# A retention step's products issued in two parts around the up products (retention, ELU layer and gated layer on one core)

## The chip, the core and the metric

One core of a Trainium2 chip runs the whole program. The metric is the device time of one execution in microseconds; the time before is the median of three runs. The engines are TensorE (PE, with its weight loads as PEld), VectorE (DVE), ScalarE (ACT), GpSimd (POOL) and SyncE (SP), which issues the DMAs. Each takes its instructions in the order in which the program issues them.

## What is computed

```python
# retention: 4 sequences, 8 heads, 576 positions, 64 wide
scores = q @ k.T / sqrt(64)
ret = scores * Dmat            # Dmat[i, j] = gamma_h ** (i - j) for i >= j, else 0
x = (ret @ v)                  # heads side by side: 2304 tokens x 512
# first layer, 512 -> 2048 -> 512
h = x @ w_in
x = where(h > 0, h, exp(min(h, 0)) - 1) @ w_out
# second layer, 512 -> 1536 -> 512
out = (sigmoid(x @ w_gate) * (x @ w_val)) @ w_o2
```

All is 32-bit. Products of the two layers are made of three products of high and low parts; those of the retention are plain 32-bit products.

## The kernel before

The retention runs in 18 steps (`NSTEP`), 9 for each pair of sequences: four chunks of 128 positions of one sequence, four of the other, and a last step that holds the last 64 positions of both. `c` is the chunk's number in its sequence; `last` marks steps 8 and 17. A step holds all eight heads, and a chunk is worked as two halves of 64 positions (`X`), so that every product is 64 x 64 x 64, four of which fit on PE side by side. In the class `Step`:

- `load` fetches q, k and v of a step (one DMA; six DMAs for a last step), `scale` (line 256, POOL) multiplies v by the decay.
- `scores` (PE, 32 products into the PSUM tile `ts`), `causal` (line 271, DVE) masks them into `a`.
- `sums` (PE, 32 products of k and v into the first 256 columns of the PSUM tile `to`; none in a last step), `states` (lines 292 to 297: two adds on DVE, or a copy on ACT and an add, then a scaling on POOL) makes of them the state for the next step.
- `inter` (PE, 32 products of a state and q into the other 256 columns of `to`; 16 where `c` is 0) and `outs` (PE, 32 products of `a` and v, added onto them) give the step's outputs. All small products are issued at line 259. `inter` issues its halves in two orders, and after its first half a no-op on SP (line 312, `swept`) waits for that half; the first product that adds onto it waits for the no-op.
- `x_scaled` (line 331 on DVE out of `to`, then a cast on ACT, line 336) and `x_low` (line 339 on DVE) give the high and low part of x for 128 tokens; `x_low` also issues on SP the DMA that keeps x (line 343).

`block(n)` writes out the order for step n: state products of n, scores of n + 1, outputs of n, sums of n + 1, the mask, the loads of a later step (`loads_at`; step 13 issues step 17's six), the scaling of the outputs, the states of n + 1, the scaling of v of n + 2, and x's low part.

The first layer begins beside it. Its stage loop runs s = 0, 1, ...; for s below 18 a pass works 256 tokens (two steps) against one 128-wide part of the hidden layer. `ups` (class `FF`) makes the hidden values: 12 products of 128 x 128 x 256 into the PSUM tile `h` (line 358), two ACT operations (lines 369, 370), one on DVE (line 373), a cast on ACT and the low part on POOL (lines 107, 108). `downs`, two passes later, adds them into `acc` (12 products, lines 112 to 114); every second pass the sums are copied out (line 407). A pass with even s takes x of steps s and s + 1 and the next pass the same two; and from s = 4 to 15 `block(s + 2)` stands ahead of `ups`. The calls of `stage()` run, in passes 6, 9, 12, 15 and 16, the conversion of a weight in pieces: ACT lines 152 and 153 at the top, DVE lines 155 and 156 behind the up products, DVE line 159 behind the two ACT operations, DVE line 161 in the down products, and a cast (ACT) and a subtraction (POOL) at the top of the next pass. The order on each engine is the order of these calls; nothing plans it otherwise.

Of the kernel before, what the change touches and what calls it, by code (L numbers as in the profile page):

```python
# [19 lines left out]
B, H, S, D = 4, 8, 576, 64  # L20
# [9 lines left out]
NSTEP = (B // 2) * NS  # L30
# [10 lines left out]
AHEAD = 2  # L41
LATE = 4
# [10 lines left out]
def retention_elu_glu(  # L53
# [25 lines left out]
    class Ring:  # L79
# [5 lines left out]
        def more(self, pool, n):  # L85
            self.homes += [(pool, f"{self.name}{len(self.homes) + i}") for i in range(n)]
# [29 lines left out]
    def warm_up(n):  # L116

        h = h_bank()
        for i in range(n):
            pe.matmul(h[:, :256], warm[:, :128], warm, start=True, stop=True)  # L120

    def after(ins, other):

        tc.add_manual_dep(ins.ins, other.ins.name, mybir.DependencyInfo(
            mybir.DependencyClass.Sync, mybir.DependencyReason.DATA), reason="row tiles")
        return ins
# [8 lines left out]
    class Weight:  # L135
# [3 lines left out]
        def load(self, raw=None):  # L139
            self.ours = raw is None  # L140
            self.raw = raw_free.popleft() if self.ours else raw
            sp.dma_start(out=self.raw, in_=self.src.bitcast(I32))
# [76 lines left out]
    class Step:  # L219
# [51 lines left out]
            dve.tensor_tensor(out=self.a, in0=ts[:, :, : NP * HC].rearrange("j h (p i) -> j h p i", p=NP),  # L271
                              in1=tri.unsqueeze(1).unsqueeze(1).to_broadcast([128, 2, NP, HC]), op=ALU.mult)

        def sums(self, start=False):

            if self.last:
                return
            for p in range(NP):
                for h in range(2):
                    for X in range(2):  # L280
                        r, d = slice(64 * X, 64 * X + 64), slice(64 * h, 64 * h + 64)
                        self.mm(to[d, X, D * p : D * p + D], self.k[r, p, d], self.v[r, p, d], start and p == 0)

        def states(self):

# [60 lines left out]
    class FF:  # L346
# [41 lines left out]
        def downs(self, stage):  # L388
            sums, n = self.sums(), self.n
            g, w = [self.gt[:, i, :n] for i in range(2)], W["o", self.f].w  # L390
            for i, a in enumerate(sums):
                c = slice(i * 128, i * 128 + 128)
                mm3(a, w[:, 0, c], w[:, 1, c], *g, self.first and not (self.half and i % 2), self.last, self.half)
                if i == len(sums) // 2 - 1:
                    stage()
            if self.last:
                self.evac(sums)
# [373 lines left out]
    with tc.manual_schedule():  # L771
# [8 lines left out]
        to = ps_r.tile([128, 2, 512], F32, name="to")  # L780
# [12 lines left out]
        steps = [Step(n) for n in range(NSTEP)]  # L793
# [6 lines left out]
        for X in range(2):  # L800
            r = slice(64 * X, 64 * X + 64)
# [17 lines left out]
        loads_at = {}  # L819
# [3 lines left out]
        def block(n):  # L823

            more = n + 1 < NSTEP
            steps[n].inter()
            if more:
                steps[n + 1].scores()
            steps[n].outs()
            if more:  # L830
                steps[n + 1].sums()
                steps[n + 1].causal()
            for load in loads_at.get(n, []):
                load()
            steps[n].x_scaled()
            if more:
                steps[n + 1].states()
                if n + 2 < NSTEP:
                    steps[n + 2].scale()
            steps[n].x_low()  # L840

        def stages(chain, n):
            for _ in range(n):
                next(chain)
# [5 lines left out]
        steps[0].scores()  # L850
        steps[0].causal()
        warm_up(WARM[1])
        steps[0].sums(True)
        steps[0].states()
        steps[1].scale()
        stages(w0, 1)
        steps[0].inter()
        steps[1].scores()
# [4 lines left out]
        for load in loads_at[0]:  # L863
            load()
        steps[0].x_scaled()
        stages(w2, 1)
        stages(w0, 1)
        steps[0].x_low()
        stages(w0, 2)
# [21 lines left out]
        for i, w in enumerate(weights[4:8]):  # L891
            s = a + 6 + (i * (b - a - 6)) // 4
# [30 lines left out]
        def park():  # L923
            for g in (2, 3):
                parked_y[g] = dpool.tile([128, KB * N[g]], F32, tag=f"y{g}", name="y")
                sp.dma_start(out=parked_y[g], in_=y_of[g])
            two, t = (ypool.tile([128, 2048], I32, tag=f"y{g}", name="more") for g in (2, 3))
            more_raws[:] = two[:, :1024], two[:, 1024:]
            extra.update({3 + i: t[:, i * DM : i * DM + DM] for i in range(3)})
            raw_shut.clear()  # L930
            raw_free.extend(more_raws)
# [36 lines left out]
        def convert(w, **engines):  # L968

            name = name_of[id(w)]  # L970
            last = 2 if isinstance(w, Sums) else 4
            for n, _ in enumerate(w.chain(**engines)):
                if n == 3 and w not in weights[:7]:
                    more()
                if n == last and w not in weights[:8]:
                    done.append([name, 3])
                yield
# [8 lines left out]
        def save(all_=False):  # L986
            for d in done:
                d[1] -= 1
            while done and (all_ or done[0][1] < 0):
                n = done.pop(0)[0]  # L990
                w = W[n].w
                copies[n] = dpool.tile(list(w.shape), F32, tag="".join(map(str, n)), name="c")
                sp.dma_start(out=copies[n], in_=w.bitcast(F32))
# [42 lines left out]
        for s in range(end):  # L1036
            if halves is not None:
                next(halves, None)
            chain = halves = None
            if s in conv:  # L1040
                chain = halves = made[name_of[id(conv[s])]] = convert(conv[s])
                if conv[s] is W["i", 2 * Q0 + 2]:
                    halves = None

            def stage():
                if chain is not None:
                    next(chain, None)
                if s >= begins[1] + 4:
                    next(prepared, None)
            stage()  # L1050
            if LATE <= s < NSTEP - AHEAD:
                block(s + AHEAD)
            ff[s].ups(stage, s)
            if s == 0:
                steps[2].scores()
                steps[2].sums(True)
                steps[2].causal()
                steps[2].states()
                steps[3].scale()
            if s == 1:  # L1060
                block(2)
                warm_up(WARM[4])
                block(3)
                warm_up(WARM[5])
                for _ in weights[1].chain(dve):
                    pass
            if 1 < s < LATE:
                block(s + AHEAD)
            for w in loads.get(s, []):
                w.load()  # L1070
            if s >= LAG:
                ff[s - LAG].downs(stage)
            else:
                stage()
            save()
            for i, n in enumerate(("11", "21", "22")):
                if s == begins[1] + 2 + i:
                    second.store(n)
            if s == begins[1] + 8:
                park()  # L1080
                more()
            if s == begins[1] + LAG - 1:
                ret.close()
                right = ctx.enter_context(tc.tile_pool(name="right", bufs=1, side="right"))
                e_tile.more(right, 3)
                e_tile.n = 5
                g_tile.more(right, 2)
                t_tile.more(right, 1)
                s_tile = Ring("s", right, 2, [128, 2, 2, DM], F32R)
                ps_acc = ctx.enter_context(tc.tile_pool(name="ps_acc", bufs=1, space=bass.MemoryType.PSUM))  # L1090
                ps_u = ctx.enter_context(tc.tile_pool(name="ps_u", bufs=1, space=bass.MemoryType.PSUM))
                acc_bank = Ring("acc", ps_acc, 4, [128, 512], F32)
                u_bank = Ring("u", ps_u, 2, [128, 512], F32)
# [79 lines left out]
        for pair in (first, second):  # L1173
# [3 lines left out]
            for q in range(Q0, QN):  # L1177
                hooks = {}
                calls = 7 + len(todo) + (not last_q)
                if not last_q:  # L1180
# [3 lines left out]
                    if q == QN - 1:  # L1184
                        reload(second.sums)
                        restore(("i", 2 * Q0), ("i", 2 * Q0 + 1), ("z", Q0))
                        p = second
# [8 lines left out]
                else:  # L1196
# [10 lines left out]
                    back = [("o", 2 * q), ("o", 2 * q + 1)]  # L1207
# [36 lines left out]
        for which, pair in enumerate(pairs):  # L1244
            for f in range(FB):
# [11 lines left out]
                back = [(n, f + 1) for n in "vgs" if f + 1 < FB and (which or f + 1 in EARLY)]  # L1257
# [28 lines left out]
                if which and f == 2:  # L1286
                    free.extend((8, 9))
                    two = y_tile(4).rearrange("p (i t) -> p i t", i=2)
# [70 lines left out]
def build(nc, arrays):  # L1359
    args = [  # L1360
        nc.dram_tensor(f"in_{n}", a.shape, mybir.dt.from_np(a.dtype), kind="ExternalInput").ap()
        for n, a in arrays.items()
    ]
    args.append(nc.dram_tensor("out_0", (NT, DM), F32, kind="ExternalOutput").ap())
    with tile.TileContext(nc) as tc:
        retention_elu_glu(tc, *args)
# [12 lines left out]
```

## Time and profile before

| | |
|---|---|
| median of three runs | 895.14 us (895.12 to 895.22) |
| the profiled execution | 894.47 us, of which the span of the profile is 892.7 us |
| PE busy | 864.8 us (97%), 6430 matmuls |
| DVE, ACT, POOL busy | 670.0, 460.0, 411.0 us |
| chain that ended last | PE 77%, DVE 11%, ACT 4%, DMA 3%, issue 2%, POOL 1% |

Times in the profile are microseconds from the start of its span. A row gives a start, a length, the engine, the line, what is written and read, and how often; in brackets stands how long the engine had been idle and who released it. "Issue" is time in which an engine waited for nothing that the profile shows.

### The profile page before, as it was taken

To read this page: it belongs to the slowest core of one execution; us is meant where nothing else is said; L and a number is where in the kernel's file an instruction comes from. 1 tells how busy PE (TensorE), PEld (TensorE's weight loads), DVE (VectorE), ACT (ScalarE), POOL (GpSimd) and SP (SyncE) were. 2 spreads that over 40 slices of the span, in tenths; PEclk is the share of its full clock that TensorE was granted. 3 is DMA by queue.
4 is the path that set the end of the run, shared out by engine and by line. 5 is a ranking of instruction groups with operands and counts; after the bars stand their busy time and mean duration, and the time that the engine had idled before them with its cause. 6 is when DMAs were issued, how large, how long until landed. Compare 5 with 4: busy or idle time off the path is not lost.

```text
span 892.7 us, 16282 instructions
## 1 busy us (share of the span) xinstructions
PE 864.8 (97%) x6430; PEld 733.3 (82%) x6430; DVE 670.0 (75%) x971; ACT 460.0 (52%) x829; POOL 411.0 (46%) x327
## 2 busy tenths in 40 slices
PE   7899999999999999999999999999999999999998
PEld 5788888878888888888778788888887888888886
DVE  4767758679999977887886989579966654786675
ACT  2344566467667655666564665455534335343331
POOL 2255635545466643565541556245434243434353
PEclk9999999999999999999999999999999999999999
DMA  9976627934655496889782666545564565554332
GB/s 340 263 241 208 184 87 245 368 118 141 203 199 213 167 407 251 307 331 336 270 310 96 258 221 225 213 171 190 205 245 180 186 208 220 212 189 189 119 118 94
DMA packets 63868, 194.83 MB, mean 218 GB/s; under 512 B 9904, under 2 KB 19120, under 8 KB 57392
## 3 DMA queue, kind: packets, MB, share of 16 engines
q1 hardware_dynamic: 62384, 192.30, 60.5%
q10 hardware_dynamic: 1408, 1.49, 0.5%
q8 instruction: 50, 0.82, 0.4%
q14 instruction: 26, 0.21, 0.1%
HBM read 127.19 MB, written 66.58 MB: 217 GB/s over the span
## 4 chain that ended last, share of the span: by engine, by line
PE 77%; DVE 11%; ACT 4%; DMA 3%; issue 2%; POOL 1%; ACTq 0%; SPq 0%; DVEq 0%; POOLq 0%
PE u L112 12%; PE u L113 12%; PE u L114 12%; PE acc L112 8%; PE acc L113 8%; PE acc L114 8%; PE tile L112 3%; PE tile L113 3%; PE tile L114 3%; PE to L259 3%; PE h L358 2%; DVE y L442 2%; DMA y<-y 1%; DVE t L155 1%; DVE t L159 1%
## 5 line engine op out<-in xcount | busy, mean ns | idle before, releaser
L108 POOL TENSOR_TENSOR g<-e,g 128x512 fp32r<-128x512 f32 x95 | 133.3, 1408 | 225.2 <-ACT g L107 200.4
L112 PE MATMUL u<-x,s 128*128 128x512 f32 x288 | 114.5, 398 | 2.8 <-ACT u L492 1.7
L114 PE MATMUL u<-x,s 128*128 128x512 f32 x288 | 114.0, 396 | 0.0
L113 PE MATMUL u<-x,s 128*128 128x512 f32 x288 | 113.6, 395 | 0.0
L112 PE MATMUL u<-x,w 128*128 128x512 f32 (+1 forms) x264 | 98.8, 374 | 3.9 <-DVE e L512 2.5
L113 PE MATMUL u<-x,w 128*128 128x512 f32 (+1 forms) x264 | 98.4, 373 | 0.0
L114 PE MATMUL u<-x,w 128*128 128x512 f32 (+1 forms) x264 | 97.9, 371 | 0.0
L107 ACT CAST g<-e 128x512 fp32r<-128x512 f32 x101 | 61.8, 621 | 59.9 <-DVE e L567 37.9
L108 POOL TENSOR_TENSOR w<-t,w 128x512 fp32r<-128x512 f32 x37 | 51.1, 1381 | 40.5 <-ACT w L107 36.9
L112 PEld LDWEIGHTS u<-x,s 128*128 128x128 f32 x288 | 54.1, 188 | 16.3 <-ACT u L492 2.6
L114 PEld LDWEIGHTS u<-x,s 128*128 128x128 f32 x288 | 54.1, 188 | 13.1
L113 PEld LDWEIGHTS u<-x,s 128*128 128x128 f32 x288 | 54.2, 188 | 11.8
L112 PE MATMUL acc<-g,w 128*128 128x512 f32 (+1 forms) x176 | 60.7, 345 | 3.0 <-DVE y L407 2.0
L112 PEld LDWEIGHTS u<-x,w 128*128 128x128 f32 x264 | 49.8, 189 | 14.0 <-DVE e L512 3.3
L114 PE MATMUL acc<-g,w 128*128 128x512 f32 (+1 forms) x176 | 60.3, 342 | 0.3 <-DVE w L108 0.2
L113 PE MATMUL acc<-g,w 128*128 128x512 f32 (+1 forms) x176 | 60.2, 342 | 0.0
L728 DVE TENSOR_TENSOR y<-y,tile 128x512 f32<-128x512 f32 x76 | 51.2, 680 | 10.0 <-PE tile L114 9.7
L764 DVE TENSOR_TENSOR y<-y,acc 128x512 f32<-128x512 f32 x58 | 39.0, 682 | 26.2 <-PE acc L114 26.1
L114 PEld LDWEIGHTS u<-x,w 128*128 128x128 f32 x264 | 49.7, 188 | 9.0
L113 PEld LDWEIGHTS u<-x,w 128*128 128x128 f32 x264 | 49.8, 189 | 8.0 <-DVE x L451 0.3
L644 DVE TENSOR_TENSOR y<-y,acc 128x512 f32<-128x512 f32 (+1 forms) x68 | 39.6, 606 | 19.7 <-PE acc L114 17.9
L113 PE MATMUL acc<-w,g 128*128 128x512 f32 (+1 forms) x152 | 54.4, 358 | 0.0
(217 smaller groups left out, 2433.3 us busy)
## 6 DMA issues: line engine op xcount, KB each, us to landing
w<-c SPq DMA_DIRECT2D x72, 512.0 KB, 6.3
c<-w SPq DMA_DIRECT2D x48, 512.0 KB, 5.0
s<-c SPq DMA_DIRECT2D x22, 1024.0 KB, 6.6
c<-s SPq DMA_DIRECT2D x18, 1024.0 KB, 5.0
in<-in_ain SPq DMA_DIRECT2D x12, 1024.0 KB, 5.9
y<-y SPq DMA_DIRECT2D x8, 1024.0 KB, 6.3
raw<-in_w_in SPq DMA_DIRECT2D x12, 512.0 KB, 4.8
c<-x SPq DMA_DIRECT2D x12, 512.0 KB, 7.8
```

The costliest lines, as they stand in the source:

```text
L107: act.copy(hi, src)
L108: lo_engine.tensor_tensor(out=lo, in0=src, in1=hi.bitcast(F32), op=ALU.subtract)
L112: pe.matmul(out_, wh, xh, start=start, stop=False, skip_group_check=shared)
L113: pe.matmul(out_, wh, xl, start=False, stop=False, skip_group_check=shared)
L114: pe.matmul(out_, wl, xh, start=False, stop=stop, skip_group_check=shared)
L155: dve.tensor_scalar(out=f, in0=f, scalar1=LEAST, scalar2=MOST, op0=ALU.max, op1=ALU.min)
L259: return pe.matmul(out_, w, x, start=start, stop=True, skip_group_check=True)
L358: pe.matmul(h, w[:, a, c[k]], x[:, b, k, t], start=i + k == 0, stop=i == 2 and k == KB - 1)
L442: dve.tensor_tensor(out=self.f32(name), in0=self.f32(a), in1=self.f32(b), op=ALU.subtract)
L644: dve.tensor_tensor(out=out_, in0=out_, in1=a, op=ALU.add)
L728: dve.tensor_tensor(out=y, in0=y, in1=a, op=ALU.add)
L764: dve.tensor_tensor(out=o, in0=o, in1=a, op=ALU.add)
```

## The change

`block` is split for the passes s = 4 to 15. `front(n)`, ahead of the up products, issues the state products of step n, the scores and the sums of step n + 1, its mask and its states. `back(n)`, between the up and the down products, issues the outputs of step n, the loads, the scaling of the outputs and cast of x, the scaling of v of step n + 2 and x's low part. The sums are now the first to write `to` behind the state products: their first product takes over the wait for the no-op on SP, and where the step has `c` 0 (no state products in half 0) they start that half's bank. `block` stays for passes 1 to 3.

```diff
--- before.py
+++ after.py
@@ -271,7 +271,7 @@
             dve.tensor_tensor(out=self.a, in0=ts[:, :, : NP * HC].rearrange("j h (p i) -> j h p i", p=NP),
                               in1=tri.unsqueeze(1).unsqueeze(1).to_broadcast([128, 2, NP, HC]), op=ALU.mult)
 
-        def sums(self, start=False):
+        def sums(self, starts=(), behind=None):
 
             if self.last:
                 return
@@ -279,7 +279,10 @@
                 for h in range(2):
                     for X in range(2):
                         r, d = slice(64 * X, 64 * X + 64), slice(64 * h, 64 * h + 64)
-                        self.mm(to[d, X, D * p : D * p + D], self.k[r, p, d], self.v[r, p, d], start and p == 0)
+                        ins = self.mm(to[d, X, D * p : D * p + D], self.k[r, p, d], self.v[r, p, d], X < len(starts) and starts[X] and p == 0)
+                        if behind:
+                            after(ins, behind.swept)
+                            behind.swept = behind = None
 
         def states(self):
 
@@ -839,6 +842,24 @@
                     steps[n + 2].scale()
             steps[n].x_low()
 
+        def front(n):
+            more = n + 1 < NSTEP
+            steps[n].inter()
+            if more:
+                steps[n + 1].scores()
+                steps[n + 1].sums((not steps[n].c,), steps[n])
+                steps[n + 1].causal()
+                steps[n + 1].states()
+
+        def back(n):
+            steps[n].outs()
+            for load in loads_at.get(n, []):
+                load()
+            steps[n].x_scaled()
+            if n + 2 < NSTEP:
+                steps[n + 2].scale()
+            steps[n].x_low()
+
         def stages(chain, n):
             for _ in range(n):
                 next(chain)
@@ -850,7 +871,7 @@
         steps[0].scores()
         steps[0].causal()
         warm_up(WARM[1])
-        steps[0].sums(True)
+        steps[0].sums((True, True))
         steps[0].states()
         steps[1].scale()
         stages(w0, 1)
@@ -1048,12 +1069,15 @@
                 if s >= begins[1] + 4:
                     next(prepared, None)
             stage()
-            if LATE <= s < NSTEP - AHEAD:
-                block(s + AHEAD)
+            two = LATE <= s < NSTEP - AHEAD
+            if two:
+                front(s + AHEAD)
             ff[s].ups(stage, s)
+            if two:
+                back(s + AHEAD)
             if s == 0:
                 steps[2].scores()
-                steps[2].sums(True)
+                steps[2].sums((True, True))
                 steps[2].causal()
                 steps[2].states()
                 steps[3].scale()
```

## Rows read from the trace of the kernel before

**Rows 1.** Windows by stage: busy us of each engine and instructions, granted clock, DMA share.
```profile
core 0: us, PE busy (x) PEld busy (x) DVE busy (x) ACT busy (x) POOL busy (x), PEclk, DMA share, GB/s
...
52.50:118.00 65.50, 62.31 (x1640) 59.38 (x1640) 42.06 (x73) 33.05 (x81) 33.00 (x35) 1.00 0.68 208
```
**Rows 2.** Chain that ended last, 38 to 130 us: start, us, what.
```profile
63.43 1.01 PE to L259 x29
...
67.30 1.93 issue
...
71.16 0.72 PE to L259 x13
...
98.97 1.01 PE to L259 x29
...
100.51 0.93 PE to L259 x62
...
104.51 1.03 PE to L259 x28
...
107.55 1.03 issue
...
111.47 1.01 PE to L259 x29
```
**Rows 3.** Windows, between the two restarts; DMA queues, 40 to 125 us (packets, MB, share).
```profile
69.20:108.57 39.37, 38.10 (x1024) 36.36 (x1024) 28.99 (x51) 19.73 (x48) 21.55 (x23) 1.00 0.67 204
...
q8 instruction: 15, 0.25, 1.1%
```
**Rows 4.** Timeline of PE, first rows of groups: start, us, engine, line.
```profile
89.40 0.22 PE L259 MATMUL to<-in 64*64 64x64 f32 x1
...
90.02 1.70 PE L358 MATMUL h<-x,w 128*128 128x256 f32 x12
91.56 0.28 PE L112 MATMUL acc<-g,w 128*128 128x256 f32 x1
...
93.09 0.79 PE L259 MATMUL to<-in,y 64*64 64x64 f32 x13
...
95.20 0.69 PE L259 MATMUL to<-y 64*64 64x64 f32 x32 [0.22 <-POOL y L256]
95.83 1.70 PE L358 MATMUL h<-x,w 128*128 128x256 f32 x12
```
**Rows 5.** Timelines of POOL, PE and DVE around one pass's up products.
```profile
58.88 0.72 POOL L108 TENSOR_TENSOR g<-d,g 128x256 fp32r<-128x256 f32 x1
59.56 1.05 POOL L256 TENSOR_TENSOR y<-y,vt 128x512 f32<-128x512 f32 x1
...
60.30 1.70 PE L358 MATMUL h<-x,w 128*128 128x256 f32 x12
...
62.96 0.42 DVE L373 SCALAR_TENSOR_TENSOR d<-d,h 128x256 f32<-128x256 f32 x1 [0.32 <-ACT d L370]
...
63.90 0.73 POOL L108 TENSOR_TENSOR g<-d,g 128x256 fp32r<-128x256 f32 x1 [3.29 <-ACT g L107]
```
**Rows 6.** Timeline of DVE: a conversion beside a busy POOL, and passes 15 and 16.
```profile
68.58 0.84 DVE L155 TENSOR_SCALAR t<-t 128x512 f32<-128x512 f32 x1
...
71.25 0.41 DVE L373 SCALAR_TENSOR_TENSOR d<-d,h 128x256 f32<-128x256 f32 x1
...
118.18 0.69 DVE L331 TENSOR_TENSOR e<-to,cq_sb 128x512 f32<-128x512 f32 x1 [1.61 <-PE to L259]
...
120.17 0.42 DVE L155 TENSOR_SCALAR t<-t 128x512 f32<-128x512 f32 x1
...
121.69 0.41 DVE L373 SCALAR_TENSOR_TENSOR d<-d,h 128x256 f32<-128x256 f32 x1
```
**Rows 7.** Timeline of SP: the last step's loads (six) and the store of x.
```profile
95.05 0.92 SPq L248 DMA_DIRECT2D in<-in_ain  x2
...
99.11 0.56 SPq L343 DMA_DIRECT2D x<-e  x1
```
**Rows 8.** Timeline of PE: the down products of pass 16.
```profile
123.33 0.39 PE L112 MATMUL acc<-g,w 128*128 128x256 f32 x1 [0.72 <-DVE y L407]
```

## The prediction

> **What bounds the kernel now.** I read the page first, then the windows by stage, then PE's own waits and the chain of waits, and last the timelines of single engines. TensorE (PE) is busy nearly everywhere, so a change counts only by what it adds to or takes from PE's queue. The change touches the twelve passes s = 4 to 15 of the stage loop, from 52.5 to 118 us. There PE is busy 62.31 of 65.50 us at the full granted clock, DVE 42, ACT 33, POOL 33 [rows 1]: PE is the bound, and some 3.2 us are to be won if every gap closed.
>
> The chain view shows where the gaps are. An undisturbed pass takes 5.54 us from one step's state products to the next (98.97 to 104.51). Two passes take longer, 7.73 us (63.43 to 71.16) and 6.96 us (104.51 to 111.47), and each holds an "issue" piece in the up products, 1.93 and 1.03 us [rows 2]: excesses of 2.19 and 1.42, together **3.6 us**. PE waits for no engine there. Between the two restarts, 69.20 and 108.57 us, lie exactly 1024 matmuls and 1024 weight loads, 2048 instructions or 8 times 256, and the instruction queue moved 15 packets of some 16 KB from 40 to 125 us, at 64 B each just 256 instructions [rows 3]. So I read both gaps as PE running out of loaded instructions. A pass of before sends 128 small products, 256 instructions, in one burst of 2.5 us (98.97 to the end of the 0.93 at 100.51, [rows 2]), which is where such a load comes too late.
>
> The only other gap of size: step 14's sums wait 0.22 us for POOL's scaling of v [rows 4].
>
> **The change, part by part.**
> A pass was: state products, scores, outputs, sums, up products, down products. It becomes: state products, scores, sums, up products, outputs, down products. The number of instructions stays; the outputs and all that hangs on them move behind the up products.
>
> (1) *Two more switches between 64x64 and 128x128 products per pass.* In line, outputs and sums take 0.93 us for 62 of their 64 products [rows 2], so outputs cost 0.47. Sums, which lead into the up products, cost 0.62 (89.40 to 90.02), and a group that stands alone 0.63 (95.20 to 95.83). Up products take 1.54 to the downs, downs 1.53 to the next small group [rows 4]. The outputs leave a slot of 0.47 and take one of 0.62 elsewhere: +0.15 us a pass, 12 passes: **+1.8 us**, all of it on PE. The pass becomes 5.69. Bounds: 0 (PE hides it in a gap) to 3.6 (twice, if both edges cost what the sums' one edge does).
> [...]
>
> (2) *Scaling of v comes behind the up products' work on POOL.* Of the moved part, every instruction counts: DVE's scaling of the outputs and x_low, ACT's cast of x, POOL's scale of step n+2, SP's loads and the store of x. The scale was ahead of POOL's subtraction for g; now it is queued behind it, and it feeds the sums one pass later. From the first up product to that subtraction are 3.60 us (60.30 to 63.90), to the scale behind it 0.68 (58.88 to 59.56), the scale takes 1.05 [rows 5], and from the sums to the next up products are 0.62 [rows 4]: 5.95 us round, with no lag between engines counted, against 5.69 on PE. So POOL's scale becomes the loop that sets the pass, by 0.26. Sums with a scale from the pass before are in s = 6 to 13, eight passes: 2.1. In two of these (steps 9 and 13, first of a sequence) PE has 16 state products less, 0.72 against 1.01 us [rows 2], so PE waits about 0.25 more in each: 0.5. **+2.6 us**. Bounds: 0 (POOL early enough) to 4 (0.2 of lags more in each pass). The 0.22 of before is within this.
>
> (3) *DVE's scaling of the outputs comes behind its work for the up products.* State products of the next step overwrite the outputs, so they wait for it. DVE does the up products' op at 2.66 after their start (60.30 to 62.96), 0.42 long [rows 5]; the scaling takes 0.69 [rows 6]. Done at 3.77; the state products are due at 1.53 + 0.62 + 1.53 = 3.68 [rows 4]. So 0 to 0.1 a pass, which hides under (2). But in s = 6, 9 and 12 a weight's conversion puts three ops ahead of that op on DVE: 2.67 us from first start to the op behind them (68.58 to 71.25) beside a busy POOL, 1.52 (120.17 to 121.69) beside an idle one [rows 6]. DVE reaches them about 1 us after the first up product (an estimate: two state adds, each with half the elements of a 0.69 scaling, are ahead), so the op starts at 2.5 to 3.7 in place of 2.66: 0 to 1.0 late. POOL has one state scaling in that time, so I take the lower middle, 0.4, which both the state products and POOL's loop then pay: **+1.3 us** for three passes (0 to 3).
>
> (4) *A semaphore step on SP's queue.* The sums' first product now waits for a no-op on SP that waits for the first half of the state products. It was the outputs that waited. Queued ahead of it on SP are the loads of the pass before and the store of x, both now later. Mostly that is one load and the store, done in time. But step 13 issues the last step's six loads: from 95.05 to the store's end at 99.67, 4.62 us of SP's queue [rows 7]. They start when step 13's outputs end, some 0.7 after those start (0.62 and a lag), so the no-op is passed at 5.3 after the outputs' start. The sums are due at 0.62 + 1.53 + 1.54 = 3.7 (98.97 to 100.51 being the last term, [rows 2]). 1.6 late, 0.2 of which (2) has counted: **+1.4 us** (0 to 2).
>
> (5) *The end.* In s = 15 the outputs of step 17 come one stage later, and s = 16's up products need their x (scaling, cast, low part: 2.0 us, 118.18 to the op behind them at 120.17, [rows 6]) while PE now offers only the down products in between. By (3) x is whole at 3.77 + 1.3 = 5.1 after the up products began; the next ones begin at 3.7 and need the low part some 0.4 later: about 1 us lost. Against that, DVE's conversion ops move into its idle 1.61 us before 118.18, and the copies for which PE waits 0.72 at 123.33 [rows 8] come earlier. I take **0** (-1 to +1).
>
> (6) *The instruction waits.* Per pass the small products now come as 96 and 32 with 12 long ones between. 256 instructions took as little as 2.5 us. Now a pass of 304 leaves out 48 of them, and the most time these can hold is the up products' 1.54 (24) and 0.2 (24 small ones): 5.69 - 1.74, so at least 3.9. Both waits should go: **-3.6**. A load can still come late where DMA is full, since from one wait to the restart 2 us passed; I give back **0.5** (0 to 3.6).
>
> Sum: 1.8 + 2.6 + 1.3 + 1.4 + 0 - 3.6 + 0.5 = **+4.0 us**. After 118 us the queue is in the same order as before, so the shift should reach the end. The profiled execution took 894.47 us (span 892.7), 0.67 below the median of 895.14; on the median the forecast is **899.1 us**. What a measurement can tell from no change is 0.2%, 1.8 us.
>
> **The rivals.**
> *Faster: the instruction waits were all that mattered.* If sums come no earlier than POOL's scale (its round at most 5.69, the point from which this decides; 0.26 less than my rows give), only (1) and (6) are left: 1.8 - 3.6 = -1.8, **893.3 us**. For it: the two waits are the stretch's largest, and they lie just where the burst is broken up. Against it: every term of the POOL round is a measured start. Chance 0.18.
> [...]
> *No difference.* The POOL round holds, but conversion ops find POOL idle and SP's six loads issue faster or later than I think: 1.8 + 2.6 - 3.6 = +0.8, **895.9 us**. For it: the upper bounds of (3) and (4) come from rows beside a busy POOL and a busy DMA. Against: POOL isn't idle in those passes, and six issues stay six issues. Chance 0.2.
> *Slower still: instruction loads stay late.* If lateness comes from DMA traffic alone, not from the burst, the 3.6 stay: +7.6, less what hides in the new waits, about **902 us**. Against: both fall in a pass with the whole burst behind them. Chance 0.07.
> The forecast keeps 0.55.
>
> **How the numbers follow.** The forecast's own range, with its terms' bounds, is 897 to 902. The faster rival reaches to about 893, so 893.0 to 902.0 leaves some 2 in 10 out. Faster by over 0.2% (below 893.4) takes most of the first rival: 0.16. Within 0.2% is the second rival and the near ends of the first and of the forecast: 0.23. Slower: 0.61.
>
> **What would show it.** Right: passes of 5.9 to 6 us; PE's sums waiting for POOL's line 256 in most passes; a wait of over 1 us at step 15's sums for SP; no "issue" pieces of 1 us in the up products; x waited for at s = 16. Wrong: passes of 5.7 with no POOL wait (the faster rival), "issue" pieces as before (the slower one), or a PE that waits for the outputs' scaling in every pass, which I price at nothing.

## The result, and the profile after

The changed kernel takes **906.33 us** (median of 4 runs, 905.10 to 908.59) against 895.13 of the kernel before (4 runs, 893.44 to 895.22): **1.0134 times, 95% interval 1.0118 to 1.0149**. Slower was forecast, but by 4.0 us; it is 11.2. One run of g1 below took 1213.74 us at a granted clock of 0.655 and is left out of its numbers. The profiled execution took 906.92 us, span 905.1, which is 12.45 more than the 894.47 of before, at a mean granted clock of 0.996 (before: 1.0).

I look first at what PE waits for in the changed stretch (line waited at, releaser: us in total, times, longest). Code lines stand three higher than before (358 is now 361, 312 is 315):

```profile
PE to L259 <- issue: 2.1, 1, 2.1
PE to L259 <- SPq L315: 1.7, 1, 1.7
PE h L361 <- ACT x L339: 0.5, 1, 0.5
PE to L259 <- POOL in L256: 0.5, 1, 0.5
```

Two waits are large: one for nothing that the profile shows ("issue", as in [rows 2]) and SP's no-op. They don't make 12 us. The chain that ended last shows the rest (start, us, what):

```profile
67.09 1.63 PE h L361 x12
68.72 0.61 PE to L259 x29
69.33 2.07 issue
71.40 0.33 PE to L259 x3
...
72.04 0.12 PE acc L113
...
72.74 0.21 PE acc L112
...
108.79 0.69 PE to L259 x32
109.48 2.46 PE h L361 x12
...
114.81 1.01 PE to L259 x29
...
116.82 1.62 PE h L361 x12
118.44 0.62 PE to L259 x32
119.07 0.32 PE acc L112
...
120.69 1.01 PE to L259 x29
```

Three things are to be seen. **The pass:** an undisturbed one, from 114.81 to 120.69, is 5.88 us, against 5.54 of [rows 2]. The up products hold 1.62 us up to the outputs, the outputs 0.62, the down products 1.63 (119.07 to 120.69). In [rows 4] the first and the last were 1.54 and 1.53. **The long wait:** 2.07 us, now inside step 8's outputs. **The slow products:** at 72.74 a down product takes 0.21 us where it took 0.12 at 72.04, and the up products at 109.48 take 2.46 in place of 1.62. The windows say why (columns as in [rows 1]; the column after POOL's is the granted clock, then DMA's share):

```profile
60.00:68.00 8.00, 8.00 (x214) 7.50 (x210) 5.34 (x7) 4.33 (x11) 2.67 (x3) 1.00 1.01 344
...
72.35:75.75 3.40, 3.40 (x53) 3.18 (x52) 1.40 (x3) 1.24 (x2) 0.93 (x2) 0.50 0.29 82
...
106.80:109.85 3.05, 1.39 (x54) 1.21 (x47) 1.29 (x3) 1.22 (x2) 0.00 (x0) 1.00 0.96 171
109.90:113.30 3.40, 3.40 (x44) 3.06 (x43) 2.70 (x7) 0.80 (x2) 0.67 (x1) 0.50 0.76 162
```

The granted clock is 0.50 for 3.4 us twice, each time about a microsecond after PE resumed from one of the two long waits. In the profile of before the clock is 1.00 throughout this part ([rows 1]). The first row shows how full DMA is ahead of the first wait.

What ended that wait stands in the trace's records of the instruction queue. From 60 to 72 us it moved one packet of 16 KB (DMA queues as in [rows 3]):

```profile
q8 instruction: 1, 0.02, 0.5%
```

It ran from 69.00 to 69.97, 9.3 us behind the end of the packet ahead of it, and PE restarted at 71.40, 1.43 behind its end. In the kernel before a packet ends at 67.76 and PE restarts at 69.22, 1.46 behind. So it is everywhere: between 55 and 125 us, 13 of the traces here have such a wait of 0.2 us or more, 20 in all, and each ends 1.2 to 1.5 us behind the end of a packet of this queue. So PE waits there for its instructions; I call them instruction waits.

The SP queue ahead of the second wait, 103.7 to 108.6 us:

```profile
103.72 1.61 SPq L248 DMA_DIRECT2D in<-in_ain  x2
105.38 0.66 SPq L250 DMA_DIRECT2D in<-in_ain  x1
106.08 1.16 SPq L248 DMA_DIRECT2D in<-in_ain  x2
107.28 0.64 SPq L250 DMA_DIRECT2D in<-in_ain  x1
108.02 0.56 SPq L346 DMA_DIRECT2D x<-e  x1
```

Six loads and the store, as in [rows 7], 4.86 us in a row; the no-op behind them ends at 108.65, and the sums start at 108.79.

Last, a loss far from the change, PE's waits from 400 to 460 us; the kernel before has only the second and third there:

```profile
PE tile L113 <- POOL g L108: 1.1, 1, 1.1
PE u L112 <- ACT u L495: 1.0, 1, 1.0
PE u L112 <- DVE e L529: 0.7, 1, 0.7
```

Lining the two traces up pass by pass, from state products to state products, gives the account of the 12.45 us (sums of excesses over an undisturbed pass; they add up to 12.4):

| term | predicted | measured |
|---|---|---|
| (1) tile switches, 12 x 0.34 | 1.8 | 4.1 |
| (2), (3) sums and state products wait for POOL and DVE | 3.9 | 1.9 |
| (4) SP's no-op at step 15's sums | 1.4 | 1.9 |
| (5) the end | 0 | 0.1 |
| (6) instruction waits | -3.1 | -1.2 |
| half clock behind two waits | none | 2.9 |
| 400 to 440 us | none | 2.4 |
| ahead of 52 us | none | 0.3 |

### The profile page after: what moved, and what is told of

Its sections match the earlier page's. It is cut to its first block, busy times and chain, and to the rows that moved or that the text cites. A ratio compares the mean times of both kernels' runs of the same rounds, so it can differ in the third digit from the quotient of the medians.

```text
span 905.1 us, 16294 instructions
## 1 busy us (share of the span) xinstructions
PE 872.8 (96%) x6430; PEld 737.8 (82%) x6430; DVE 675.6 (75%) x971; ACT 460.7 (51%) x829; POOL 406.9 (45%) x327
## 4 chain that ended last, share of the span: by engine, by line
PE 70%; DVE 14%; DMA 6%; ACT 6%; issue 2%; POOL 1%; SPq 1%; ACTq 0%; DVEq 0%; POOLq 0%
PE u L112 11%; PE u L113 11%; PE u L114 11%; PE acc L112 8%; PE acc L113 8%; PE acc L114 8%; PE to L259 3%; PE tile L112 3%; PE tile L113 2%; PE tile L114 2%; DMA raw<-in_w_o 2%; PE h L361 2%; DVE y L445 2%; DMA y<-y 1%; DVE t L161 1%
## 5 line engine op out<-in xcount | busy, mean ns | idle before, releaser
L112 PE MATMUL acc<-g,w 128*128 128x512 f32 (+1 forms) x176 | 62.3, 354 | 2.2 <-DVE y L410 1.2
L114 PE MATMUL acc<-g,w 128*128 128x512 f32 (+1 forms) x176 | 60.6, 345 | 0.3 <-DVE w L108 0.2
L113 PE MATMUL acc<-g,w 128*128 128x512 f32 (+1 forms) x176 | 60.5, 343 | 0.0
L113 PE MATMUL acc<-w,g 128*128 128x512 f32 (+1 forms) x152 | 54.4, 358 | 0.0
L112 PE MATMUL acc<-w,g 128*128 128x512 f32 (+1 forms) x152 | 54.3, 357 | 0.0
```

What stands on the lines that cost most here:

```text
L112: pe.matmul(out_, wh, xh, start=start, stop=False, skip_group_check=shared)
L113: pe.matmul(out_, wh, xl, start=False, stop=False, skip_group_check=shared)
L114: pe.matmul(out_, wl, xh, start=False, stop=stop, skip_group_check=shared)
```

## The experiments

Each time stands against runs of the kernel before on the same chip. The changed kernel itself stands at 1.0134 above and at 1.0098 when it was run again (e4), so that a difference of some 3 us between the times of two variants shows nothing by itself; such steps are read from the traces. Edits are to the changed kernel, except where the text says that they are to the kernel before.

**Does the order matter, or the place of the outputs?** Both parts ahead of the up products: the outputs behind the sums, but no up products between.

```diff
                 front(s + AHEAD)
+                back(s + AHEAD)
             ff[s].ups(stage, s)
-            if two:
-                back(s + AHEAD)
```

> Front and back part both ahead of the up products: the new order inside a step (sums ahead of the outputs, states early) without the split. Theory (the split itself costs: 0.34 us a pass for two more switches, SP's wait at step 15's sums, late x and late scale): all of this goes, passes of 5.55 us again, no SP wait; 893 to 897 us. Rival (the new order of sums and outputs is what costs, through the wait of sums on the no-op and the outputs on DVE): time stays above 900 us and PE waits for SP or DVE in most passes.

Measured 908.5 us (907.34 to 910.37), ratio 1.0141 [1.0118, 1.0164]: no better than the split, though the two added switches are gone. PE's waits from 45 to 145 us:

```profile
PE to L259 <- DVE st L299: 8.9, 8, 1.9
PE to L259 <- DVE y L299: 3.4, 3, 1.1
```

The outputs write the same PSUM tile `to` out of which DVE reads the sums for the states; directly behind the sums they wait for that. The split hides this wait under the up products. To see the order without it, the state adds went behind the outputs:

```diff
                 steps[n + 1].causal()
-                steps[n + 1].states()
...
             steps[n].x_scaled()
+            if n + 1 < NSTEP:
+                steps[n + 1].states()
...
                 front(s + AHEAD)
+                back(s + AHEAD)
             ff[s].ups(stage, s)
-            if two:
-                back(s + AHEAD)
```

> The joined kernel (front and back both ahead of the up products) with the states' adds issued behind the outputs and their scaling, as before the change. Theory (in the joined kernel each step's outputs waited 1.3 us for the state adds, which read the other half of the same PSUM tile): these waits go, passes of 5.55 us, 894 to 897 us. Rival (the no-op on SP, or the sums' place, costs): over 900 us.

Measured 900.28 (900.07 to 901.24), 1.006 [1.0047, 1.0073]. The state waits go and an undisturbed pass is 5.55 us again, as before, so the 0.34 belongs to the outputs' new place. The time expected isn't reached, because an instruction wait of 3.3 us (below) stands in the up products, with half clock from 70.75 to 74.16, POOL and SP still hold the sums up, and 2.2 us go at 400 to 440 us:

```profile
PE h L361 <- issue: 3.3, 1, 3.3
...
PE to L259 <- POOL y L256: 0.7, 1, 0.7
PE to L259 <- SPq L315: 0.6, 1, 0.6
```

**POOL's scale.** Back to its place ahead of the up products:

```diff
                 steps[n + 1].states()
+            if n + 2 < NSTEP:
+                steps[n + 2].scale()
...
             steps[n].x_scaled()
-            if n + 2 < NSTEP:
-                steps[n + 2].scale()
```

> The changed kernel with POOL's scale of v of step n + 2 moved back ahead of the up products, behind the states. Theory (with passes of 5.89 us on PE the POOL round of 5.95 is nearly level): 0.5 to 1.5 us gained against the changed kernel, passes 8 and 9 0.1 to 0.2 us shorter at the sums. Rival (POOL's late scale is the main cost, as predicted at 2.6 us): 2.5 us or more gained in the stretch.

Measured 905.93 (902.76 to 906.89), 1.0108 [1.0085, 1.0131]. The sums' waits for the scale go; in two passes with a conversion PE's state products now wait 0.9 and 0.7 for DVE's scaling of the outputs. The shift at 140 us is 7.0 us where the changed kernel's is 10.0, but this trace has no half clock (its run, at clock 1.0, is the 902.76; the others, at 0.995 to 0.996, took 905.33 to 906.89), though its instruction wait is 2.3 us. Without the 2.9 us of half clock the changed kernel's would be some 7.1, so moving the scale gained next to nothing: DVE's waits took the place of POOL's.

**SP's loads.** Step 17's six loads go behind the no-op:

```diff
-            for load in loads_at.get(n, []):
+            for load in loads_at.get(n, []) if n != 13 else []:
...
                 front(s + AHEAD)
+                if s + AHEAD == 14:
+                    for load in loads_at[13]:
+                        load()
```

> The changed kernel with only the last step's six loads moved from the back part of step 13 behind the front part of step 14, so that the no-op of step 14 is not queued behind them on SP. Theory: the wait of 1.9 us at step 15's sums goes, and with it the stretch of half clock that follows it at 110 to 113 us (1.4 us): 3.0 to 3.5 us gained against the changed kernel. Rival (the half clock comes from the small products themselves, not from the wait): the wait goes but the clock still falls, 1.9 us gained.

Measured 904.95 (903.94 to 905.55), 1.0102 [1.0087, 1.0117]. The wait for SP is gone, and with it the second half-clock stretch: from 100 to 114 us PE is busy 13.87 of 14.00 us at 1.00, while the first one, behind an instruction wait of 2.2 us, is still there (0.52 from 72.5 to 76.0). The time doesn't show the 3.0 to 3.5 us that were expected (the changed kernel, run beside it as e4, took 904.17), and the half clock may have stayed away by chance, as e4 shows.

**The changed kernel again.** 64 no-ops ahead of PE's first warm-up were to shift its instructions:

```diff
+        for _ in range(64):
+            pe.nop()
         warm_up(WARM[0])
```

> The changed kernel with 64 no-ops added to PE's queue ahead of the first warm-up products, which shifts where blocks of 256 instructions end by 64. Theory (PE waits for a block of instructions to be loaded): the wait of 2.07 us at step 8's outputs leaves its place by 64 instructions (to the up products or the sums ahead of it), and its size changes, or it goes and another comes; the restart points still lie multiples of 256 instructions apart. Rival (a transfer or a semaphore behind the outputs): the wait stays at the same products of pass 6 with 2 us.

They left nothing in PE's queue (16294 instructions as without them, and the first restart behind 1371 matmuls again), so this is the changed kernel once more: 904.17 (901.74 to 908.13), 1.0098 [1.0063, 1.0134]. Its four runs are 901.74 and 901.92 at a granted clock of 1.0, 906.43 and 908.13 at 0.996 and 0.994. The half clock doesn't come in every execution, and the runs with and without it lie 4.5 to 6.4 us apart; without it the change costs some 8 (of the kernel before, the run with the highest clock there, 0.999, took 893.96).

A run's mean clock doesn't say where the half clock stood, though. This trace (of the 906.43) has it from 11.4 to 14.9 us, ahead of everything that was changed, and from 72.9 to 76.3, at the instruction wait of 2.5 us; behind SP's wait it has none:

```profile
PE to L259 <- SPq L315: 1.5, 1, 1.5
...
110.20:114.20 4.00, 4.00 (x86) 3.73 (x87) 3.06 (x7) 0.91 (x3) 0.67 (x1) 1.00 0.80 167
```

An early stretch like this, between 11 and 16 us, is in the traces of e1, e3, f4, h2 and g3 (the kernel before), too. With it the passes begin 1.0 to 2.6 us later than in the first trace of before, without it -0.1 to 0.5. So part of the 4.5 to 6.4 is no cost of the change.

**What an instruction wait depends on.** The kernel before with 16 more idle products early on, 32 instructions:

```diff
-WARM = 24, 14, 12, 16, 10, 14
+WARM = 24, 14, 12, 16, 26, 14
```

> The kernel before with 16 more warm-up products, 32 more PE instructions, at a place where PE waits 2 us anyway. Theory (PE stops where a block of 256 instructions ends): the waits in the up products of passes 6 and 13 restart 32 instructions earlier in the pass, among the sums of the small products ahead of them, or go and others come at such a place; counted in PE's instructions the restart points stay multiples of 256 apart. Rival (a semaphore or a weight): the waits stay within the up products. Time within 2 us of before.

Measured 901.13 (899.07 to 902.73), 1.0059 [1.0042, 1.0077]: some 5 us slower. Its trace (of the 902.73) has a span 8.3 longer than the first of before: 2.6 ahead of the passes, with an early half clock there, 3.1 in the passes and 2.6 at 400 to 440 us (below); how much of it the shift itself costs isn't shown. The wait, now 3.3 us, falls into the small products, with half clock from 72.7 to 76.1. Windows of f4, from the start to the first restart and from there to the second:

```profile
0.00:72.01 72.01, 56.45 (x1372) 49.47 (x1372) 39.04 (x68) 24.29 (x51) 21.94 (x27) 0.98 0.78 262
...
72.00:109.62 37.62, 36.34 (x896) 34.74 (x896) 26.46 (x47) 18.70 (x45) 19.79 (x21) 0.95 0.74 215
```

and of the changed kernel to its only restart:

```profile
0.00:71.39 71.39, 55.90 (x1371) 48.46 (x1371) 43.24 (x73) 25.78 (x55) 22.68 (x29) 1.00 0.81 264
```

PE restarts behind the same count of matmuls, 1371 or 1372, whatever product stands there (the kernel before: 1372 too), and the restarts lie 7 x 256 instructions apart here (896 matmuls and as many loads) as 8 x 256 in [rows 3]. So it is the position in the queue that waits; its length is another matter (3.3 us here, but 3.3 in f3, too, where nothing is shifted). Then DMA traffic: the kernel before with step 12's load (1 MB) one pass later, so that pass 5 issues none.

```diff
-            loads_at.setdefault(m - 5 if m < 13 or m == 14 else m - 3 if m == 13 else m - 4, []).append(steps[m].load)
+            loads_at.setdefault(m - 5 if m < 12 or m == 14 else m - 3 if m == 13 else m - 4, []).append(steps[m].load)
```

> The kernel before with one 1 MB load (step 12's) issued in step 8's block, where none is, in place of step 7's. Theory (the 2.19 us wait in pass 6 is a block of PE's instructions that queues behind bulk transfers, the DMAs being full from 60 to 67 us): that wait shrinks to under 1 us, 1 to 2 us faster than before, 893 to 894 us. Rival (the burst of 128 small products is what outruns the load, whatever the DMAs do): the wait stays at 2 us and the time is that of before.

Measured 893.44 (891.76 to 896.10), 0.9991 [0.9979, 1.0004]: not shown faster. Pass 6 no longer waits, but another position does, 1.2 us at 78 us, five times 256 instructions ahead of a small one of 0.3 at 105; that of pass 13 stays (1.0). The same edit on the changed kernel:

> The changed kernel with step 12's load issued one step later, and nothing else. Theory (the instruction wait at step 8's outputs comes from the load's traffic, and the half clock at 72 to 76 us follows from that wait): both go, 2.3 + 1.4 = 3.7 us faster than the changed kernel, 902 to 903 us, the wait for SP at step 15's sums and what follows it stay. Rival (the half clock does not depend on the wait): 2.3 us or less.

Measured 902.72 (901.44 to 904.02), 1.0092 [1.0078, 1.0106]. From 64.5 to 68 us DMA's share falls from 0.97 in the changed kernel to 0.66; the instruction wait and the half clock behind it are gone. The instruction queue moves two packets from 60 to 72 us where the changed kernel has one, the first from 65.65 to 67.06:

```profile
q8 instruction: 2, 0.03, 1.2%
```

All five traces with this load later (f1, f2, g2, h2, h3) have no wait at the position of pass 6, and the ten others all have one there, 0.4 to 3.3 us. SP's wait and the half clock behind that stay:

```profile
104.00:106.00 2.00, 0.54 (x20) 0.57 (x24) 0.55 (x1) 1.02 (x2) 0.00 (x0) 0.86 1.03 209
106.00:109.00 3.00, 3.00 (x36) 2.88 (x28) 2.09 (x5) 0.00 (x0) 0.66 (x1) 0.52 0.97 199
```

**Is it PE's idleness that costs the clock?** The same kernel, and SP's wait filled with idle products:

```diff
                 steps[n + 1].scores()
+                if n == 14:
+                    warm_up(14)
                 steps[n + 1].sums((not steps[n].c,), steps[n])
```

> The changed kernel with step 12's load one step later, and with 14 idle products of 128 x 128 x 256 (1.5 us) put on PE where it waits for SP at step 15's sums. Theory (the clock falls to half because PE stands still there): the wait for SP is filled, the clock stays at 1.0 from 100 to 112 us, 1 to 1.5 us faster than without them, 901.2 to 901.7 us. Rival (the small products themselves let the clock fall): half clock again and the same time.

Measured 902.48 (901.11 to 903.88), 1.0082 [1.0065, 1.01]. The clock stays at 1.00, and PE is busy all the time:

```profile
104.00:108.00 4.00, 4.00 (x87) 3.48 (x84) 2.25 (x6) 1.25 (x4) 0.66 (x1) 1.00 1.09 229
```

From the first split pass to 140 us this trace gains 1.4 us on g2's, and the six runs have clocks of 0.998 and above, where four of g2's five are at 0.996 or 0.997. That fits the idea. It isn't shown: e4's clock stayed at 1.00 behind a wait of 1.5 us that nothing filled. Nor do the runs show that it pays; the medians differ by 0.2 us only, within their spread.

**All of it mended.** The scale in front, the six loads late and step 12's load later (the edits of e2, e3 and g2 together):

```diff
+            loads_at.setdefault(m - 5 if m < 12 or m == 14 else m - 3 if m == 13 else m - 4, []).append(steps[m].load)
...
                 steps[n + 1].states()
+            if n + 2 < NSTEP:
+                steps[n + 2].scale()
...
+            for load in loads_at.get(n, []) if n != 13 else []:
...
```

> The changed kernel with the scale of v ahead of the up products, the last step's six loads one pass later and step 12's load one step later. Theory (what then is left of the change is the two switches, 0.34 us a pass, 12 passes, 4.1 us): no wait over 1 us in passes 4 to 15 but the first one for the scale, no half clock, 898 to 900 us. Rival (waits come back at other places, or the loss lies elsewhere): 903 us or more.

Measured 900.05 (898.77 to 900.56), 1.0053 [1.0041, 1.0065]. No half clock, no instruction wait of size, undisturbed passes of 5.89; what still holds PE up from 45 to 145 us is DVE:

```profile
PE to L259 <- DVE e L334: 2.4, 3, 1.0
PE to L259 <- issue: 0.2, 1, 0.2
```

They stand behind the outputs of passes 6, 9 and 12, where the conversion's op is ahead of the scaling, beside POOL's scale:

```profile
68.85 1.23 POOL L256 TENSOR_TENSOR in<-in,vt 128x512 f32<-128x512 f32 x1
...
69.21 1.42 DVE L159 CUSTOM_DVE_ANT_0 t<-raw,t 128x1024 uint16<-128x1024 uint16 x1
...
70.88 0.68 DVE L334 TENSOR_TENSOR e<-to,cq_sb 128x512 f32<-128x512 f32 x1
```

So with the other waits gone the split is still 4.8 us slower: 4.1 of switches, 2.4 of DVE's waits and 0.5 for POOL in pass 4, with 1.5 lost at 400 to 440 us (below), less the 3.6 of gaps that before had. Moving the conversion's DVE ops behind the second part, too:

```diff
-            ff[s].ups(stage, s)
+            ff[s].ups((lambda: None) if two else stage, s)
             if two:
                 back(s + AHEAD)
+                stage()
+                stage()
```

> The mended kernel with the weight conversion's DVE operations of passes 6, 9 and 12 issued behind the back part, so that the scaling of the outputs isn't queued behind them. Theory (state products waited there for DVE's scaling of the outputs, 1.03, 0.75 and 0.81 us): these three waits go, 2 to 2.6 us faster than the mended kernel, about 897.5 us; what is left against before is the switches, 4.1 us a stretch, less the instruction waits of before. Rival (the conversion then is late itself, and its weight or the next pass's mask waits): no gain.

> The kernel with the conversion's DVE operations behind the back part once more, for a trace that is not disturbed. Theory: the waits for DVE's scaling of the outputs are gone, and the 2 to 4 us that it is slower than the mended kernel stand in one or two other waits of over 1 us (an instruction block, or the conversion's end) between 50 and 140 us. Rival: spread over all passes.

Measured 904.04 (four runs, 901.50 to 904.86), 1.0103 [1.0087, 1.0119]: slower than without it, where about 897.5 was expected; a single run of the same kernel, the traced one (h2), took 902.87. There the state adds and the copy of `acc` come late behind the conversion instead (2.8, 2.6 and 0.7 us of PE's time; of the 2.6, 1.2 were there in f2):

```profile
PE to L259 <- DVE st L299: 2.8, 3, 1.4
PE acc L112 <- DVE y L410: 2.6, 2, 1.4
```

**The loss at 400 to 440 us.** The kernel before unchanged, for the spread of that stretch, and with seven more DVE instructions at the start, in case it comes from their count:

> The kernel before, unchanged, for a second trace of it. Theory: waits of some 2 and 1 us in the up products of passes 6 and 13 again, at the same instructions, no half clock between 50 and 140 us, and the time from 380 to 440 us within 0.5 us of the first trace. Rival (the 2.4 us that the changed kernel lost there are an accident of single executions): it differs by 1 us or more.

```diff
-        dve.memset(warm, 0.0)
+        for _ in range(8):
+            dve.memset(warm, 0.0)
```

> The kernel before with seven more instructions at the start of DVE's queue (a small fill, repeated), the number by which the changed kernel's DVE queue is longer. Theory (the 1 to 2.8 us which the changed kernels lose between 400 and 440 us come from DVE's instructions, a few more of them, being loaded at another moment): the second trace loses over 1 us there against the first trace of before. Rival (the few instructions are no cause): under 0.5 us there, time of before.

The kernel before: 895.44 (894.77 to 896.21), 1.0008 [0.9996, 1.002], that stretch within 0.1 us of the first trace. (Its instruction waits stand at the same two positions, but are 1.9 and 0.3 us, not 1.9 and 1.0 as in the first trace; in h1 they are 1.8 and 0.2. The trace of g3 has half clock from 11.5 to 14.9 and from 25.1 to 28.6 us, none from 50 to 140.) With the seven: 894.69 (893.83 to 895.58), 0.9993 [0.9982, 1.0003], 0.3 us lost at 400 to 440. The idea falls.

Across the traces the loss is 1.3 to 2.9 us in e1, e2, e3, e4, f2, f3, g2 and h3, all with the new order of sums and outputs, and 0.4 or less in the kernel before, f1, g3 and h1. But f4, a variant of the kernel before, loses 2.6, and h2, with the new order, none (-0.5): so the order doesn't set it. The traces that lose come to that stretch 3.3 us or more later than the kernel before, those that don't within 1 us of it, h2 (8.9 later) apart. What sets it is open.

## Why the prediction was wrong

The direction was right and the size wrong: 4.0 us forecast, 11.2 measured, beyond the range's 902.

**(1), the switches, was mis-sized: 1.8, measured 4.1**, and past its upper bound of 3.6. I took the up products' 1.54 and the down products' 1.53 to stay as they were whatever follows and precedes them. But at these groups, too, an edge to the other tile size costs about 0.1. The outputs themselves cost 0.62 in place of 0.47, as I said; the up products ahead of them 1.62 in place of 1.54; the down products behind them 1.63 in place of 1.53: 0.15 + 0.08 + 0.10 = 0.33 a pass, with the 5.88 of a pass against 5.54. f3 has 5.55 with the same order of sums and outputs and no outputs behind the up products. The trace of before held the price. Pass 16's down products stand between two groups of their own size and take 1.44 (119.57 to 121.01); with one edge twelve such products take 1.53 or 1.54, with two now 1.62 or 1.63.

```profile
119.57 0.28 PE L112 MATMUL acc<-g,w 128*128 128x256 f32 x1
...
121.01 1.60 PE L358 MATMUL h<-x,w 128*128 128x256 f32 x12
```

**(6), "both waits should go", failed by half.** The wait of pass 6 stayed (2.07 against 1.93), at the same position of the queue, and inside step 8's outputs, where no full burst of small products had been ahead. That of pass 13 went; but g3 and h1, without the change, have only 0.3 and 0.2 there, so the -1.2 of the table holds for this pair of traces. My "at least 3.9 us" for 256 instructions was right for PE, but the block came later than that here, with DMA full: its share is 1.01 from 60 to 68 us, and from the end of one packet to the start of the next are 9.3 us (59.68 to 69.00), in g2 5.9 (59.77 to 65.65). g2, with the load later and DMA's share at 0.66 from 64.5 to 68 us, has no wait. That is the mechanism of the rival that I gave 0.07, for one of the two waits. That PE's instructions come in blocks of 256 the traces bear out: the restarts of before, f4 and f1 lie 8, 7 and 5 times 256 instructions apart, and in before the instruction queue moved 8 packets of 16 KB for the 2048 instructions between the restarts and 50 (0.82 MB) for the 12860 matmuls and weight loads of the whole span, some 64 B for each.

**What I didn't foresee: half clock behind a wait.** A wait of 1.7 or 2.1 us of PE was followed by 3.4 us at half clock: 2.9 us in this trace. e3 and g2 each took one wait away and its half clock went with it; h3 kept the wait's length and filled it, and the clock stayed. Not every wait does so: the instruction waits of before and g3 (1.93), h1 (1.8) and e2 (2.3) had none, and SP's wait had none in e2 (1.3) and e4 (1.5). As e4 is the changed kernel itself, e3 and h3 don't exclude chance. What decides is open; the traces of after and e4, one program, have clocks of 0.50 behind SP's wait of 1.7 us and 1.00 behind that of 1.5, so the program alone doesn't set it.

**(2) and (3), POOL and DVE, came out at half: 3.9 against 1.9.** I had POOL's round, 5.95, stand against a pass of 5.69; against the 5.88 that PE takes by itself it adds little. The terms were not independent: what (1) lacked, (2) had. Of the 1.9, 0.5 is a wait for POOL in pass 4, ahead of the eight passes that I counted, and it is there with the scale in front, too (e2, f2). The sums' waits for POOL "in most passes" came in four, 0.1 to 0.2 each. When the scale was moved in front, DVE's scaling behind the conversion was next, 0.7 to 1.0 a time, 2.4 in f2, near the upper bound that I had for (3). (My three times 0.4 there are 1.2, not 1.3.)

**(4) and (5) were right.** SP's no-op cost 1.9 against 1.4, by the six loads as described, and e3 shows it. At s = 16 x was waited for, 0.5 us, and the wait for the copies of [rows 8] went: 0.1 together against 0.

**"After 118 us the shift should reach the end" failed**: 2.4 us more are lost between 400 and 440 us, in code that the change doesn't touch. f4 loses as much there without the change. No run here settles why.

The faster rival, 893.3, needed passes of 5.7 with both instruction waits gone. f2 is nearest to its condition, with hardly an instruction wait (0.2 us) or a wait for POOL, and passes are still 5.89: (1) alone decides against it. No version here is shown to beat the kernel before; the nearest is f1.

## What to carry to other kernels

When a group of small products is moved between groups of another tile size, price the entry of the moved group and of the one behind it, and the exit of the one ahead (0.15, 0.10 and 0.08 us a pass here); one edge of a row is not the whole. A group that stands between its own size shows what it takes without edges (1.44 us here). Before a gap of PE is charged to the instructions just ahead of it, see whether it moves with their count from the start or with the DMA traffic; here it moved with both (f4; f1 and g2). PE's waits of 2.07 and 1.7 us were followed by half clock in the changed kernel's trace, which cost some 1.4 us more each, and one of 1.93 in the kernel before was not; so in a mean over runs the price of such a wait is its length and what follows it, but a run's mean clock doesn't tell where the half clock stood (e4). A no-op that guards on a DMA queue is to be priced with the DMAs issued there ahead of it: here it stood behind six loads and a store, 4.86 us.

## What the runs showed of the hardware that was not expected

- Stretches of 3.4 us at a granted clock of 0.50 at PE waits of 1.6 to 3.3 us, but not at all of them. In the changed kernel's trace they begin 1.0 and 1.1 us behind the end of the wait, in e3, e4, f3, f4 and g2 from 0.2 us ahead of it to 0.7 behind. A down product took 0.21 us there against 0.12.
- PE's restarts lie a multiple of 256 instructions apart where a trace has more than one of size (8 x 256 before, 7 x 256 in f4, 5 x 256 in f1), and each comes 1.2 to 1.5 us behind the end of a 16 KB packet of the instruction queue.
- Twelve 128x128 products take 1.44 us between groups of their own tile size, 1.53 or 1.54 with 64x64 products on one side, 1.62 or 1.63 with them on both.
